# Row-tiled products in two passes: the body's full-height matmuls become pairs of 64-row matmuls on two PSUM banks

## The chip, the cores and the metric

One NeuronCore of one Trainium2 chip. The metric is the time of one execution on the device in microseconds (us). The kernel before takes 799.0 us, the median of three runs (797.24, 799.0 and 799.35).

## The reference

For each of eight batches (3200 tokens, 256 channels, inputs `u`, `v`, `z` in float32):

```
attn = relu(z z^T / S) ** 2            # 3200 x 3200, z has 64 columns
x    = u * (attn @ v)                  # gated attention
wq, wk = x @ w_q, x @ w_k              # 64 columns each
mixed  = (wq wk^T / sqrt(64)) @ x      # = wq @ (wk^T x), a 64 x 256 matrix in the middle
out    = relu(mixed) @ w_out
```

Two shapes of product matter here. The scores `z z^T` and the product with `wk^T x` contract over 64 values, which is half the height of TensorE's array of 128 rows. All others contract over 128 at a time.

## The kernel before

A batch's 25 blocks of 128 tokens are cut into seven groups of output columns: six of 512 tokens and one of 128 (`widths`, `LASTG` is the last). A *score tile* is a block of 128 tokens against one group. Since the scores are symmetric, a tile is made once and its mirror image is got from it by a transposing DMA (`is_turned`, tiles `tt` and `ttl`).

The work runs in **phases**, numbered `k`, in the `while groups` loop (L644 to L767); the order inside a phase is written by hand, and each engine works through its own instructions in that order. One phase does the following.

- **Scores** (`scores`, L212, matmul on L218). Three pairs of score tiles, one after the other at the head of the phase. The two tiles of a pair use the lower and the upper 64 rows of the array (`half = h * dqk`), because `zT` holds `z` twice, once in each half, and they write two PSUM banks of one `sc` tile. In 40 phases a `mix` (L431, also 64 rows) takes the place of one pair.
- **First stage** (`first_stage`, L233): relu and scale from PSUM into a float32 tile `g`. One pair of the phase is done by ScalarE (L237), the others by VectorE (L241).
- **Second stage** (`second_stage`, L247): the squares of the pairs of the phase before, as fp16 tiles `at`, on GpSimd (L256) or ScalarE (L254), then the transposing DMA (L275).
- **Second product** (`second_product`, L287, matmul on L296): blocks of `at`, `tt` or `ttl` as weights and `v` as moving operand, 256 columns a matmul, over all 128 rows. The sums of a group's four 128-token blocks stay in two PSUM banks, `acc0` and `acc1` (pool `pacc`, one buffer each), over the group's one to six phases.
- **An extra**, in about half of the phases: after the first ten matmuls of the second product comes either `keys_and_heads` (L568: `projections` on L344, `heads` on L382, in a few cases `side_mix` or `side_proj`) or `proj` (L472). Each takes a `ps` tile of two banks from a pool of three (`pps`) that the score pairs also use.

When a group closes, the matmuls for `acc0` are put ahead of those for `acc1`, and **the gate** (`gate`, L318, VectorE on L322) multiplies each bank by `u` as soon as that bank is finished. `heads` needs the keys `kx`, which a transposing DMA (`turn_keys`, L364) and a GpSimd copy (`double_keys`, L371) prepare from an earlier extra.

Of the kernel before, what the change touches and what calls it, by code (L numbers as in the profile page):

```python
# [9 lines left out]
FP16 = mybir.dt.float16  # L10
# [6 lines left out]
def kernel(  # L17
# [194 lines left out]
    def scores(p0):  # L212
        pair = tiles[p0 : p0 + 2]
        sc = ps_tile("sc")
        for h, (b, gi, ti) in enumerate(pair):
            gs, gw = starts[gi], widths[gi]
            half = h * dqk
            nc.tensor.matmul(  # L218
                out=sc[:, h, 0:gw],
                lhsT=zT[b][half : half + dqk, ts(ti, P)],  # L220
                rhs=zT[b][half : half + dqk, ds(gs, gw)],
                start=True,
                stop=True,
            )
        return sc
# [7 lines left out]
    def first_stage(p0, sc, on_act):  # L233
        g = pg.tile([P, 2, W], FP32, tag="g", name="g")
        for hs, w in pieces(p0):
            if on_act:
                nc.scalar.activation(  # L237
                    out=g[:, hs, 0:w], in_=sc[:, hs, 0:w], func=RELU, scale=GSCALE
                )
            else:  # L240
                nc.vector.tensor_scalar(  # L241
                    out=g[:, hs, 0:w], in0=sc[:, hs, 0:w], scalar1=0.0,
                    scalar2=GSCALE, op0=AOP.max, op1=AOP.mult,
                )
        return g
# [33 lines left out]
    def weights(b, gi, ti, j):  # L279

        if (b, gi, ti) in made:
            at, at0 = made[b, gi, ti]
            return at[:, ds(at0 + j * P, P)]
        gj = group_of(ti)
        return turned[b, gj, gi][:, j, ti - starts[gj] // P, :]

    def second_product(b, gi, rows_, first, last):  # L287

        nj = widths[gi] // P
        halves = range((nj + 1) // 2)  # L290
        if first:
            for half in halves:
                accs[half] = acc_tile(half, f"acc{half}")

        def one(ti, j):
            nc.tensor.matmul(  # L296
                out=accs[j // 2][:, ds((j % 2) * D, D)],
                lhsT=weights(b, gi, ti, j),
                rhs=vs[b][:, ti, :],
                start=(first and ti == rows_[0] and j % 2 == 0),  # L300
                stop=(last and ti == rows_[-1] and (j % 2 == 1 or j == nj - 1)),
            )

        todo = []
        if last:
            for half in halves:
                for ti in rows_:
                    for j in range(2 * half, min(2 * half + 2, nj)):
                        todo.append(lambda ti=ti, j=j: one(ti, j))
                run = todo.pop()  # L310
                todo.append(lambda run=run, half=half: (run(), gate(b, gi, half)))
        else:
            for ti in rows_:
                for j in range(nj):
                    todo.append(lambda ti=ti, j=j: one(ti, j))
        return todo

    def gate(b, gi, half):  # L318
        if half == 0:
            xs[b, gi] = px.tile([P, 4, D], FP16, tag="x_sb", name="x_sb")  # L320
        n = min(2, widths[gi] // P - 2 * half)
        nc.vector.tensor_mul(  # L322
            out=xs[b, gi][:, 2 * half : 2 * half + n, :].rearrange("p n d -> p (n d)"),
            in0=accs[half][:, 0 : n * D],
            in1=us[b, gi][:, 2 * half : 2 * half + n, :].rearrange("p n d -> p (n d)"),
        )
        if 2 * half + n == widths[gi] // P:
            us.pop((b, gi))
            turn_x(b, gi)
# [10 lines left out]
    def projections(b, gi, w, out, start=True):  # L340

        gw = widths[gi]
        for ac in range(ND):
            nc.tensor.matmul(  # L344
                out=out,
                lhsT=w[:, ac, :, :].rearrange("p t h -> p (t h)"),
                rhs=xTs[b, gi][:, 0 : gw // P, ac, :],
                start=(start and ac == 0),
                stop=(ac == ND - 1),
            )  # L350

# [26 lines left out]
    def heads(b, gis, ps, stop=True):  # L378

        parts = [(gi, n) for gi in gis for n in range(widths[gi] // P)]  # L380
        for gi, n in parts:
            nc.tensor.matmul(  # L382
                out=ps[:, 1, 0:D],
                lhsT=ks[b, gi][:, n, :, :].rearrange("p a h -> p (a h)"),
                rhs=xs[b, gi][:, n, :],
                start=((gi, n) == parts[0]),
                stop=(stop and (gi, n) == parts[-1]),
            )

# [77 lines left out]

    def proj_half(b, gi, banks, half):
        js = range(2 * half, min(2 * half + 2, widths[gi] // P))
        for dc in range(ND):  # L470
            for j in js:
                nc.tensor.matmul(  # L472
                    out=banks[half][:, ds((j % 2) * D, D)],
                    lhsT=rts[b, gi][:, dc, ts(j, P)],
                    rhs=wo[:, dc, :],
                    start=(dc == 0 and j == js[0]),
                    stop=(dc == ND - 1 and j == js[-1]),
                )
# [39 lines left out]
    def side_mix(b, ps):  # L518
        for db in range(ND):
            nc.tensor.matmul(  # L520
                out=ps[:, 1, ds(D + db * P, P)],
                lhsT=hz[b % 2][:, ds(db * P, P)],
                rhs=qks[b, LASTG][:, 0:P],
                start=False,
                stop=(db == ND - 1),
            )

# [8 lines left out]
    def side_proj(b, ps):  # L536
        for dc in range(ND):
            nc.tensor.matmul(
                out=ps[:, 1, D : 2 * D],
                lhsT=rts[b, LASTG][:, dc, :],  # L540
                rhs=wo[:, dc, :],
                start=False,
                stop=(dc == ND - 1),
            )

# [21 lines left out]

    def keys_and_heads(b, gis):  # L568
# [4 lines left out]
        projections(b, gis[0], w, outs[0])  # L573
        aside = None
        if keyed:
            heads(*keyed[0], ps, stop=(len(gis) == 1 and not side))
            if len(gis) > 1:
                projections(b, gis[1], w, outs[1], start=False)
            elif side:
                aside = side.pop(0)  # L580
                aside[0](aside[2], ps)
        for gi, o in zip(gis, outs):
            projections_out(b, gi, o)
            turn_keys(b, gi)
        if keyed:
            hb, hgis = keyed.pop(0)
            heads_out(hb, hgis, ps)
            if hgis[-1] == LASTG:
                mixed_at[0] = max(mixed_at[0], now[0] - 1)
                todo_mix.extend((hb, i, db) for i in range(LASTG // 2) for db in range(ND))  # L590
                side.append((side_mix, side_mix_out, hb))
        if aside:
            aside[1](aside[2], ps)
        keyed.append((b, gis))
        keyed_at[0] = now[0]
# [46 lines left out]
    left, sizes = None, []  # L642
    gate_pending = False
    while groups:  # L644
# [17 lines left out]
        fresh = []  # L662
        for p0 in range(produced, produced + n, 2):
            fresh.append((p0, scores(p0)))
# [12 lines left out]
        for i, (p0, sc) in enumerate(fresh):  # L677
            on_act = i == act_pair and not mixing
            staged.append((p0, first_stage(p0, sc, on_act)))
        if k < 3:  # L680
            turn_first(k + 1)
# [48 lines left out]
        matmuls = second_product(b, gi, rows_, begins, closes)  # L730
        extra = None
        if mixing and todo_proj:
            mb, mg = todo_proj.pop(0)

            def extra():
                proj_out(mb, mg, proj(mb, mg), [(False, nc.sync, widths[mg] // P)])
        elif keying:
            extra = todo_between.pop(0)[1]
        elif len(groups) <= NG and todo_proj and gi < LASTG:
            mb, mg = todo_proj.pop(0)  # L740

            def extra():
                proj_out(mb, mg, proj(mb, mg), [(False, nc.sync, widths[mg] // P)])
        cut = 10 if extra else 0
        if closes and (b, gi) == (last, LASTG):
            assert not extra
            cut = 20

            def extra():
                last_gram(last, LASTG - 1, psg)  # L750

            psg = [acc_tile(1, "xtx")[:, 0:D], ps_tile("xtx")[:, 0, 0:D]]
        for fn in matmuls[:cut]:
            fn()
        if extra:
            extra()
        for x in acts[1:]:
            second_stage(*x)
        for fn in matmuls[cut:]:
            fn()  # L760
        if closes:
            group_done(k, b, gi)
# [15 lines left out]
    def query(gi, o):  # L778
        projections(last, gi, wq2, o)
# [8 lines left out]
    heads(hb, hgis, psh, stop=False)  # L788
# [59 lines left out]
```

## Time and profile before

| | |
|---|---|
| median of the runs | 799.0 us |
| profiled execution, first to last instruction (its span) | 796.6 us |
| matmuls and weight loads on TensorE | 6746 and 6746 |
| TensorE busy | 783.4 us, 98% of the span |
| VectorE, ScalarE, GpSimd busy | 485.5, 462.1, 476.1 us |
| granted TensorE clock | 0.999 |

The profiled execution has one time of its own, the span of its only core; the runs' times lie 0.6 to 2.8 us above it. Engines are PE (TensorE matmul), PEld (its weight load), DVE (VectorE), ACT (ScalarE), POOL (GpSimd) and SP (which issues most DMAs). A matmul's record runs from its start to the modelled arrival of its last column in PSUM, and records of successive matmuls overlap; what one matmul costs the engine is the distance from its start to the next start, not its duration. A group's line gives the count, the busy time, the mean duration in ns, and the idle time before it with what ended it.

### The profile page before, as it was taken

The page shows a single profiled execution, that of the slowest core. Times are in us where ns is not written, and L with a number is a line of the kernel's source. Part 1 is how long each engine was busy: PE and PEld are TensorE (multiplying, and loading weights), DVE is VectorE, ACT ScalarE, POOL GpSimd, SP SyncE. Part 2 cuts the span into 40 slices and gives each one's busy share as a digit, 9 for nine tenths or more (in the row PEclk, how much of TensorE's full clock was granted, in tenths as well). Part 3 has the DMA queues.
Part 4 walks back from the last instruction along what each step waited for, and adds up shares of the span by engine and source line. Part 5 has one row for each costly group of instructions (what it writes and reads, how often), then busy time and mean ns, then how long its engine had stood idle before and what let it go on. Part 6 is the DMA issues. An engine that isn't in the chain of part 4 may idle for free. (4 is left out here: it accounts for less than half of the span.)

```text
span 796.6 us, 16567 instructions
## 1 busy us (share of the span) xinstructions
PE 783.4 (98%) x6746; PEld 584.3 (73%) x6746; DVE 485.5 (61%) x509; ACT 462.1 (58%) x514; POOL 476.1 (60%) x350
## 2 busy tenths in 40 slices
PE   7999999999999999999999999999999999999996
PEld 4777777777777777777777777777777777777784
DVE  5755567646576566655666556775567655675514
ACT  6655556546565557555665556655556655665624
POOL 7967568646664566754667466584566555676420
PEclk9999999999999999999999999999999999999999
DMA  8999899989999989996899978999899995978625
GB/s 170 164 208 191 129 183 161 192 175 173 181 182 202 190 156 174 190 219 146 167 216 165 197 154 182 150 206 222 155 195 177 179 224 117 212 167 192 152 41 221
DMA packets 331116, 141.00 MB, mean 177 GB/s; under 512 B 310560, under 2 KB 313248, under 8 KB 331040
## 3 DMA queue, kind: packets, MB, share of 16 engines
q1 hardware_dynamic: 302768, 123.70, 78.7%
q0 software_dynamic: 28128, 15.98, 18.5%
q8 instruction: 53, 0.87, 0.5%
q10 hardware_dynamic: 144, 0.26, 0.1%
q14 instruction: 23, 0.19, 0.1%
HBM read 59.38 MB, written 26.21 MB: 107 GB/s over the span
## 5 line engine op out<-in xcount | busy, mean ns | idle before, releaser
L256 POOL TENSOR_TENSOR at<-g 128x1024 f16<-128x1024 f32 (+1 forms) x228 | 419.4, 1854 | 223.7 <-DVE g L241 154.2
L241 DVE TENSOR_SCALAR g<-sc 128x1024 f32<-128x1024 f32 (+1 forms) x330 | 376.3, 1183 | 177.2 <-PE sc L218 173.6
L296 PE MATMUL acc<-v_sb,at 128*128 128x256 f16 x3528 | 432.3, 273 | 0.0
L296 PEld LDWEIGHTS <-at 128*128 128x128 f16 x3528 | 332.3, 98 | 104.4 <-issue 60.9
L237 ACT ACTIVATE g<-sc 128x1024 f32<-128x1024 f32 x122 | 125.1, 1025 | 201.7 <-PE sc L218 201.6
L254 ACT ACTIVATE at<-g 128x1024 f16<-128x1024 f32 (+2 forms) x224 | 227.4, 1028 | 0.6 <-DVE g L241 0.6
L296 PE MATMUL acc<-v_sb,tt 128*128 128x256 f16 x1280 | 163.1, 273 | 0.0
L296 PEld LDWEIGHTS <-tt 128*128 128x128 f16 x1280 | 125.2, 98 | 14.5
L218 PE MATMUL sc<-zT 64*128 64x512 f16 x888 | 125.6, 382 | 1.6 <-ACT zT L122 0.9
L322 DVE TENSOR_TENSOR x_sb<-acc,u_sb 128x512 f16<-128x512 f32 (+1 forms) x104 | 69.4, 669 | 76.0 <-PE acc L296 73.3
L452 ACT ACTIVATE rt<-mx 128x1024 f16<-128x1024 f32 x47 | 47.9, 1024 | 65.3 <-PE mx L431 63.5
L218 PEld LDWEIGHTS <-zT 64*128 64x128 f16 x888 | 34.1, 95 | 47.1 <-issue 26.3
L371 POOL COPY kx<-kx 128x256 f16<-128x256 f16 (+1 forms) x54 | 20.1, 378 | 70.3 <-DMA kx<-qk 69.3
L507 ACT ACTIVATE fo<-fo 128x1024 f32<-128x1024 f32 (+2 forms) x44 | 43.8, 1000 | 22.6 <-PE fo L472 22.6
L472 PE MATMUL fo<-wo,rt 128*128 128x256 f16 x384 | 50.0, 273 | 0.1
L472 PEld LDWEIGHTS <-rt 128*128 128x128 f16 x384 | 37.3, 98 | 5.7 <-issue 1.3
L358 ACT CAST qk<-qk 128x512 f16<-128x512 f32 x47 | 27.5, 586 | 21.5 <-PE qk L382 12.6
L395 DVE TENSOR_TENSOR ha<-ha,qk 128x256 f32<-128x256 f32 x31 | 13.1, 421 | 32.0 <-ACT qk L358 25.9
L382 PE MATMUL qk<-x_sb,kx 128*128 128x256 f16 x191 | 28.4, 273 | 0.0
L382 PEld LDWEIGHTS <-kx 128*128 128x128 f16 x195 | 19.1, 98 | 12.0
L296 PE MATMUL acc<-v_sb,ttl 128*128 128x256 f16 x192 | 22.9, 273 | 0.0
L127 POOL DMA_DIRECT2D v_sb<-in_v_dram x35 | 20.8, 596 | 0.0
(61 smaller groups left out, 166.3 us busy)
## 6 DMA issues: line engine op xcount, KB each, us to landing
u_sb<-in_u_dram SPq DMA_DIRECT2D x48, 512.0 KB, 4.7
out_dram<-fo SPq DMA_DIRECT2D x45, 512.0 KB, 3.8
v_sb<-in_v_dram POOLq DMA_DIRECT2D x35, 320.0 KB, 6.2
zd<-in_z_dram POOLq DMA_DIRECT2D x7, 400.0 KB, 9.3
tt<-at SPq DMA_TRANSPOSE x162, 4.4
out_dram<-fo SPq DMA_DIRECT2D x5, 256.0 KB, 2.7
u_sb<-in_u_dram SPq DMA_DIRECT2D x8, 128.0 KB, 3.0
xT_sb<-x_sb SPq DMA_TRANSPOSE x56, 4.1
```

The source lines that it names most:

```text
L218: nc.tensor.matmul(out=sc[:, h, 0:gw], lhsT=zT[b][half : half + dqk, ts(ti, P)], rhs=zT[b][half : half + dqk, ds(gs, gw)], start=True, sto ...
L237: nc.scalar.activation(out=g[:, hs, 0:w], in_=sc[:, hs, 0:w], func=RELU, scale=GSCALE)
L241: nc.vector.tensor_scalar(out=g[:, hs, 0:w], in0=sc[:, hs, 0:w], scalar1=0.0, scalar2=GSCALE, op0=AOP.max, op1=AOP.mult,)
L254: nc.scalar.square(out=out, in_=g[:, hs, 0:w])
L256: nc.gpsimd.tensor_mul(out=out, in0=g[:, hs, 0:w], in1=g[:, hs, 0:w])
L296: nc.tensor.matmul(out=accs[j // 2][:, ds((j % 2) * D, D)], lhsT=weights(b, gi, ti, j), rhs=vs[b][:, ti, :], start=(first and ti == rows_[ ...
L322: nc.vector.tensor_mul(out=xs[b, gi][:, 2 * half : 2 * half + n, :].rearrange("p n d -> p (n d)"), in0=accs[half][:, 0 : n * D], in1=us[b, ...
L358: nc.scalar.copy(out=qks[b, gi][:, 0:gw], in_=out)
L382: nc.tensor.matmul(out=ps[:, 1, 0:D], lhsT=ks[b, gi][:, n, :, :].rearrange("p a h -> p (a h)"), rhs=xs[b, gi][:, n, :], start=((gi, n) == ...
L452: nc.scalar.activation(out=out, in_=ps[:], func=RELU)
L472: nc.tensor.matmul(out=banks[half][:, ds((j % 2) * D, D)], lhsT=rts[b, gi][:, dc, ts(j, P)], rhs=wo[:, dc, :], start=(dc == 0 and j == js[0]),
L507: nc.scalar.mul(out=flat_out[:, sl], in_=part, mul=FINAL_SCALE)
```

## The change

In the phases from the fourth on (`on_lanes`, 159 of 164), every product is made of 64-row matmuls. A product over 128 rows is an `Item` with one PSUM target. `lanes` emits all items of two banks with the lower 64 rows for one bank and the upper 64 rows for the other, interleaved by column position; later the same items are emitted with rows and banks exchanged, so that every bank gets both halves. Between the two passes stands one score pair, which now comes out of the head of the phase (two pairs, or a `mix` and one pair, stay there). `swap_after` makes the first weight load of the second pass wait for the last matmul of each lane of the first pass. From phase to phase the lanes keep their banks (`across`). In the built program this wait stands on a weight load; no instruction is added for it.

The 128-token group needs one PSUM bank only. Except in the last batch it is done in one pass (`is_split`, `both_lanes`): lower rows into `acc0`, upper rows into `acc1`, added up at the gate. An extra goes first in both passes, no longer after ten matmuls of the second product; what reads it follows its second pass. The gate comes after both banks: ScalarE copies `acc1` to SBUF, and VectorE multiplies `acc0` by `u`, then the copy by `u`. Score tiles of the last group are computed at full width (512 columns) and only the last 128 columns are read.

The program has 12268 matmuls in place of 6744 and as many weight loads, 55 more ScalarE copies and 7 more VectorE operations. DMAs are the same in number.

```diff
 def scores(p0):
-            gs, gw = starts[gi], widths[gi]
+            gs = min(starts[gi], S - W)
-                out=sc[:, h, 0:gw],
+                out=sc[:, h, :],
...
+    def lanes(banks, across, second):
+        todo, ends_ = [], {}
+        for lane, rows in enumerate((LOW, HIGH)):
+            at = 0
+            for i in banks[lane ^ across]:
+                todo.append((at, lane, i, rows))
+                at += width(i)
+        for _, lane, i, rows in sorted(todo, key=lambda x: x[:2]):
+            ends_[lane] = i.emit(rows, i.start and not second, i.stop and second)
+        return list(ends_.values())
+
+    def both_lanes(banks):
+        for low, high in zip(*banks):
+            low.emit(LOW, low.start, low.stop)
+            high.emit(HIGH, high.start, high.stop)
+
+    def swap_after(ends_):
+        ins = nc.tensor.nop()
+        for earlier in ends_:
+            tc.add_manual_dep(
+                ins.ins,
+                earlier.ins.name,
+                mybir.DependencyInfo(mybir.DependencyClass.Sync, mybir.DependencyReason.DATA),
+                reason="the lanes change banks",
+            )
+
+    def is_split(b, gi):
+        return gi == LASTG and b + 1 < B
...
+    def gate(b, gi):
...
+        if is_split(b, gi):
+            both = pg.tile([P, W], FP32, tag="g", name="gt")
+            nc.scalar.copy(out=both[:, 0:n], in_=accs[1][:, 0:n])
+            nc.vector.tensor_add(out=both[:, 0:n], in0=accs[0][:, 0:n], in1=both[:, 0:n])
+            nc.vector.tensor_mul(out=x[:, 0:n], in0=both[:, 0:n], in1=ug[:, 0:n])
         else:
+            if nn > 2:
+                upper = pg.tile([P, W], FP32, tag="g", name="gt")
+                nc.scalar.copy(out=upper[:], in_=accs[1][:])
+            nc.vector.tensor_mul(out=x[:, 0:n], in0=accs[0][:, 0:n], in1=ug[:, 0:n])
+            if nn > 2:
+                nc.vector.tensor_mul(out=x[:, n : 2 * n], in0=upper[:], in1=ug[:, n : 2 * n])
+        turn_x(b, gi)
...
-        for p0 in range(produced, produced + n, 2):
-            fresh.append((p0, scores(p0)))
+        pairs = list(range(produced, produced + n, 2))
+        on_lanes = k >= 3 and len(pairs) + bool(mixing) >= 2
+        between_ = [pairs.pop()] if on_lanes else []
+        fresh = [(p0, scores(p0)) for p0 in pairs]
...
+        if on_lanes:
+            split = is_split(b, gi)
+            if extra:
+                ends_ = lanes(extra[0], across, False)
+            if split:
+                both_lanes(banks)
+            else:
+                ends_ = lanes(banks, across, False)
+            for x in acts[1:]:
+                second_stage(*x)
+            for p0 in between_:
+                stage(p0, scores(p0))
+            if extra or not split:
+                swap_after(ends_)
+                across = not across
+            if extra:
+                lanes(extra[0], across, True)
+                extra[1]()
+            if not split:
+                lanes(banks, across, True)
...
         if closes:
+            gate(b, gi)
             group_done(k, b, gi)
```

## The prediction

> **What bounds the kernel now.** I read the page's first part, then who waited for whom, then TensorE's timeline around one score block.
>
> ```profile
> PE 783.4 (98%) x6746; PEld 584.3 (73%) x6746; DVE 485.5 (61%) x509; ACT 462.1 (58%) x514; POOL 476.1 (60%) x350
> ```
>
> TensorE is the bound and no other engine is near. The waits of its matmuls for other engines add up to 7 us. Its weight loads show another idle time, which nobody ends ("issue"):
>
> ```profile
> PEld L296 <- issue: 60.9, 144, 0.4
> PEld L218 <- issue: 26.3, 123, 0.5
> ```
>
> The columns are the total in us, the times and the longest. L296 loads for the second product, L218 for the scores: a gap stands at each change between the two. The timeline of PE shows it from the matmuls' side (start, length, count), then that of PEld at the same place:
>
> ```profile
> 403.11 0.49 PE L296 MATMUL acc<-v_sb,at 128*128 128x256 f16 x3
> 403.54 0.82 PE L218 MATMUL sc<-zT 64*128 64x512 f16 x6
> 404.29 0.39 PE L296 MATMUL acc<-v_sb,at 128*128 128x256 f16 x2
> ```
>
> ```profile
> 403.53 0.12 PEld L218 LDWEIGHTS <-zT 64*128 64x128 f16 x4 [0.21 <-issue]
> ```
>
> Three matmuls of 273 ns in 0.49 us: the pitch is 109 ns, so the third starts at 403.33 and the score would be due at 403.44. It comes at 403.54. The last score pair starts at 403.98, the next pair would be due 216 ns later, and L296 starts at 404.29, another 92 ns late; its second matmul follows after 119 ns, not 109, and the second score pair after 226, not 216. From the last full-height matmul to the second one behind a block of three pairs, the trace has 1078 ns; 109 + 3 x 216 + 109 is 866. A change from 128 rows to 64 and back costs **212 ns**. The waits carry it: the product goes on undisturbed between these changes.
>
> **What the change removes.** 159 phases run on lanes, so 158 round trips go (one is left around the whole stretch). 158 x 0.212 = **-33.5 us**.
>
> **The pitch of a pair on lanes.** A full-height matmul of 256 columns becomes two pairs of 64-row matmuls of which each has half of the work, so 109 ns per pair leaves TensorE's work as it was. No row has a pair of 256 columns. The nearest: two score matmuls start 3 to 4 ns apart and a pair of 512 columns takes 216 ns, as one full-height matmul of 512 does (L344: 216). Four score loads go out within 19 ns (the line of PEld above), so loads of the two halves don't queue for each other. A pair needs four instructions in 109 ns, 27 ns each:
>
> ```profile
> L520 PE MATMUL qk<-ql,hz 128*128 128x128 f16 x14 | 1.9, 219 | 0.0
> ```
>
> These fourteen come in seven couples; 1.9 us by seven is 274 ns, so a couple's second starts 55 ns after the first, load included: the same 27 ns, if only for a few instructions. The bounds are 0 (the score row) and +10 ns a pair (the 119 ns row, where weights could not be loaded ahead). I take **0**, the score row, since it has the same shape of work. There are about 5600 pairs (4883 of the second product, the rest extras), so each ns is 5.6 us: +56 at the upper end.
>
> **The gate.** Now the next group's first matmul needs both accumulator banks, and both are released late:
>
> ```profile
> L322 DVE TENSOR_TENSOR x_sb<-acc,u_sb 128x512 f16<-128x512 f32 x96 | 66.0, 689 | 66.1 <-PE acc L296 63.4 <-DMA ttl<-at 0.7
> ...
> L358 ACT CAST qk<-qk 128x512 f16<-128x512 f32 x47 | 27.5, 586 | 21.5 <-PE qk L382 12.6
> ```
>
> From the start of a group's last matmul: it ends after 273 ns, VectorE starts 37 later, takes 689, and TensorE starts 53 after VectorE's end (all measured): `acc0` is free at 1.05 us. ScalarE's copy of `acc1` (nearest row 586, L358) frees it at 0.95. Before, three score pairs with both switches covered this (first matmul on `acc0` at 0.95 us, on `acc1` at 1.17) and `acc0` was multiplied earlier anyway. Now two pairs stand there, without switches: 109 + 2 x 216 = 541 ns. In the built order,
> - 23 groups begin behind a 512-token group without an extra: 23 x 0.51 = 11.8 us;
> - 24 begin with an extra of at least 1024 columns a lane (436 ns): 24 x 0.07 = 1.7;
> - 7 follow a one-pass (128-token) group. There the score pair of the middle stands behind all matmuls, and VectorE takes its relu (1.22 us, starts at 0.53) before the gate's sum (0.42): `acc0` is free at 2.2 us, and with the output extra in that phase at 2.9. Waits of 1.0 to 1.5 us: 8.3;
> - the last 128-token group, after the lanes: 0.9.
>
> Together **+22.7 us**. VectorE and ScalarE must be idle when a group closes; by the order they are (the middle pair's relu ends about 0.3 us before the gate), and if not, it costs more.
>
> **The swap.** The wait of the second pass stands behind a score pair. Last matmul at 0, score at 109, next due at 325. The last matmul's end is seen at 273 + 40 to 55, so the load comes at 313 to 328 and the matmul 5 ns later; then one pitch is 10 longer, as after a switch. 155 swaps x 14 ns = **+2.2** (0 to 8). Queued behind this load is all of TensorE.
>
> **What becomes late next.** These places had cover before:
> - *Keys.* An extra stands first in its phase instead of after ten matmuls, 1.6 us earlier, and its results leave about 0.5 us later. `heads` needs `kx`:
>
> ```profile
> POOL kx L371 <- DMA kx<-qk: 69.3, 20, 8.1
> ```
>
>   GpSimd waits long for these transposes. In 8 of 54 cases its copy ended less than 2.1 us ahead of the first load; what is missing adds up to 6 us. Bounds 0 and 10, I take **+5**.
> - *PSUM tiles of the extras.* A phase's second score pair takes the tile that the extra of the phase before used. In short phases with two squares on ScalarE (1.05 each, after a 1.02 `mix` output) the extra's output ends at 4.6 us, and the pair is due at 4.4: about 10 places x 0.3 = **+3** (0 to 6).
> - *Unequal lanes.* The extras' two banks differ by 9984 columns in all; at 109 ns per 256 that is 4.3 us if the shorter lane idles in both passes, 0 if the second pass makes up for the first. **+3**, since the swap waits for the longer lane.
> - *Squares.* A pass goes through the blocks twice as fast, so the third pair's `at` is due 1.4 us earlier. First uses had 4.8 us (ScalarE) and 7.1 us (GpSimd) in the median, 2.3 and 3.4 at the lowest twentieth: **+1** (0 to 3).
>
> Free: the wider scores of the last group (8 tiles; the other lane takes 512 columns anyway), 55 ScalarE copies and 7 VectorE operations (58 and 61% busy), 0.7 MB more instructions.
>
> **Sum.** -33.5 + 22.7 + 2.2 + 5 + 3 + 3 + 1 = +3.4. On the profiled span, 796.6 + 3.4 = 800.0; the median of the runs stands 2.4 above that span: **802.4**, say 802. The saving is real, and the gate and the later waits eat it.
>
> **Rivals.**
> 1. *Only the gate and the swap are left over* (faster). The waits put at 5, 3, 3 and 1 share their causes: each stall of TensorE gives ScalarE, GpSimd and the DMAs time, so the next is shorter. -33.5 + 22.7 + 2.2 = -8.6: **790**. For it: the median slacks above. It decides if the four are under 3 us together; with some gates covered too, down to 785.
> 2. *Lanes do not reach 109 ns* (slower). If four instructions per 109 ns, or two loads, cannot be kept up and every pair costs what the first behind a switch does (119), it is 802 + 56 = **858**; from 3 ns a pair on the result is slower by 2% whatever else happens. For it: no row shows this rate for more than a few instructions, and the rate held over long stretches is 54 ns an instruction. Against it: the score pairs and the couples of L520. The Trainium skill, TensorE: Matmul & The Clock Gate, section Back-to-back issue gap, gives about 81 ns for each load and matmul of 128 columns in a sustained stream. By that page a pair would take 162 ns and 5600 pairs some 297 us more, an estimate. The couples' 55 ns disagree with it as far as they go.
> 3. *ScalarE or GpSimd fall behind around the gates* (slower): the copies delay the squares of the same phase, and the next group waits for them too. At 0.25 us for each of 56 groups, +14: **816**. Against it: both have 40% idle time.
> 4. *The switch cost stays*, because a load that waits for the whole array empties it as a switch does: 155 x 0.2 instead of 2.2 is +29: **831**. Against it: the load is due 12 ns after that end anyway.
>
> **How the numbers follow.** Forecast 802: 0.40 (its own range 796 to 810); rival 1, 790: 0.30; rival 2: 0.14; rival 3: 0.11; rival 4: 0.05. A measurement of this kernel tells a difference from none at about 0.3%, 2.4 us. Faster than 796.6: rival 1 and the lower edge of the forecast, 0.33. Within 796.6 to 801.4: the middle of the forecast, 0.20. Slower: 0.47. The range reaches from 786 to 822 and leaves out rivals 2 and 4.
>
> **What would show it.** Right: 109 ns from pair to pair on L291 of the changed kernel, 216 from a score pair to the next product, idle time of about 0.5 us in front of the first matmul of 23 groups, ended by VectorE, about 1 us behind the one-pass groups, and nothing over 20 ns at the swaps. Wrong: a pitch over 110 ns (rival 2), 0.1 to 0.2 us at each swap (rival 4), or no idle time at the gates; then VectorE was done earlier than I worked out, and the time is near 780.

## The result, and the profile after

| | before | after |
|---|---|---|
| median of five runs each | 798.6 us (797.24 to 799.35) | **822.6 us** (821.24 to 831.91) |
| ratio, with its 95% interval | | 1.032 (1.028 to 1.037) |
| span of the profiled execution | 796.6 us | 830.1 us (its own time: 831.9) |
| granted TensorE clock in it | 0.999 | 0.991 |

The kernel is 24 us slower; 802 us was forecast, with a range of 786 to 822. The median before is of five runs; the 799.0 us above was that of the first three. The profiled execution is the slowest of the five, so its sum is made against its own span: 33.5 us more than before. The same kernel profiled once more (`e0_again`) had a span of 825.2 us.

The first line of the page shows what has changed place. TensorE (PE) is no longer busy throughout:

```profile
PE 775.4 (93%) x12270; PEld 625.9 (75%) x12270; DVE 511.8 (62%) x516; ACT 486.5 (59%) x569; POOL 480.6 (58%) x350
```

The waits of PE name who it is idle for (total in us, times, longest):

```profile
PE fo L291 <- ACT rt L512: 15.3, 20, 1.0
PE qk L291 <- POOL kx L429: 9.5, 4, 3.4
PE acc L291 <- DVE x_sb L382: 5.4, 15, 0.4
...
PE qk L291 <- DVE g L241: 2.7, 3, 0.9
PE acc L291 <- ACT gt L381: 2.4, 8, 0.3
PE sc L218 <- DVE g L241: 2.2, 3, 0.7
PE acc L291 <- DVE gt L376: 1.2, 1, 1.2
```

This view counts from the modelled end of the matmul before (273 ns after its start), but the engine could have started the next one after 109 ns, so each wait costs 0.16 us more than it shows: the first row is 15.3 + 20 x 0.16 = 18.5 us. Waits shorter than 0.16 us are not in it at all. So I took the starts of all matmuls, with a pitch of 109 ns for 256 columns and 55 and 216 for 128 and 512, and split the span, without the 7.2 us at its end where TensorE has no more to do, in three:

| us | TensorE idle | one lane of two at work | whole array or both lanes |
|---|---|---|---|
| before | 46.3 | 3.8 | 739.3 |
| after | 71.1 | 20.2 | 731.6 |
| difference | +24.8 | +16.4 | -7.7 |

The three differences add up to the 33.5 us. The idle time by what ended it, in us:

| | before | after | predicted change |
|---|---|---|---|
| switches between 128 and 64 rows, with the long pitch behind them | 32.9 | 0 | -33.5 |
| first matmul of a group, for either bank of the accumulators | 0 | 13.9 (39 waits) | +22.7 |
| score or keys' tile behind a one-pass group, for VectorE's relu | 0 | 6.1 (8 waits) | +3, elsewhere |
| swaps, with the long pitch behind them | 0 | 2.8 | +2.2 |
| **output product, for ScalarE's mix output** | 0 | **18.5** (20 waits) | **not in the sum** |
| keys, for GpSimd's copy | 0 | 10.4 (7 waits) | +5 |
| half clock behind the three longest waits | 0 | about 5 | not in the sum |
| squares | 0 | 1.0 | +1 |
| one lane at work, at half the rate | | +8.2 | +3 |

Two single waits of 1.1 us are not in the table: one for the transposing DMA of `x_sb` in front of the keys' projection (at 47 us), one without a shown releaser (at 162 us). With them the column of after, less the 32.9, is +35.3 us, 1.8 more than the spans differ by: the half clock is an estimate, and the pitches are known to 1 ns.

**The missing row.** One of the twenty waits in PE's timeline (start, length, line, count):

```profile
399.83 0.38 PE L491 MATMUL mx<-qk,hs 64*128 64x512 f16 x2
400.04 0.39 PE L218 MATMUL sc<-zT 64*128 64x512 f16 x2
400.26 0.39 PE L291 MATMUL fo<-wo,rt 64*128 64x256 f16 x4
401.33 0.39 PE L291 MATMUL fo<-wo,rt 64*128 64x256 f16 x4 [0.67 <-ACT rt L512]
401.56 0.38 PE L291 MATMUL acc<-v_sb,at 64*128 64x256 f16 x4
401.77 0.93 PE L291 MATMUL acc<-v_sb,tt 64*128 64x256 f16 x14
```

and ScalarE's at the same place:

```profile
400.25 1.02 ACT L512 ACTIVATE rt<-mx 128x1024 f16<-128x1024 f32 x1 [0.49 <-PE mx L491]
```

The `mix` is the first thing in the phase, and ScalarE takes 1.02 us to turn its sums into `rt`. One score pair stands between the `mix` and the output product that reads `rt`, then four of its matmuls that read the older half of `rt`. The fifth would have been due at 400.26 + 0.22 = 400.48 us; it starts at 401.33, 0.85 us late. In the trace of before, two score pairs and ten matmuls stand between the `mix` and the extra (PE, then ACT):

```profile
407.02 0.39 PE L431 MATMUL mx<-qk,hs 64*128 64x512 f16 x2
407.24 0.59 PE L218 MATMUL sc<-zT 64*128 64x512 f16 x4
407.77 1.26 PE L296 MATMUL acc<-v_sb,at 128*128 128x256 f16 x10
408.87 1.04 PE L472 MATMUL fo<-wo,rt 128*128 128x256 f16 x8
```

```profile
407.45 1.02 ACT L452 ACTIVATE rt<-mx 128x1024 f16<-128x1024 f32 x1 [0.51 <-PE mx L431]
```

In 20 phases the output product reads the `rt` that the `mix` of its own phase completes. There its first load of `rt` follows the end of the mix output by only 0.29 us, and the third, the first that reads the new half, by 0.51 us. The extra moves ahead by ten matmuls (1.09 us) and a score pair (0.22 us), so it was bound to wait 0.8 us in each of these phases. The row was there, and I looked at the keys only.

The last line of PE's timeline also answers for the pitch: 14 matmuls are seven pairs in 0.93 us, and less the last pair's 0.27 that is six pitches of **109 ns**, with 14 loads among them. It holds through the whole body.

**The gate**, as worked out: the group's last pair starts at 405.18 (the end of the line at 403.98 us, less 0.27), the next group's first at 406.26, 1.08 us later where 1.05 was predicted:

```profile
403.98 1.47 PE L291 MATMUL acc<-v_sb,tt 64*128 64x256 f16 x24
405.29 0.60 PE L218 MATMUL sc<-zT 64*128 64x512 f16 x4
406.26 0.28 PE L291 MATMUL acc<-v_sb,at 64*128 64x256 f16 x2 [0.38 <-DVE x_sb L382]
```

**The half clock.** In three stretches the granted clock falls. One of them in windows of the page's kind (window, its length, busy time of PE, PEld, DVE, ACT, POOL with counts, PE clock, DMA share, GB/s), with what GpSimd waited for ahead of it:

```profile
270.00:274.00 4.00, 3.88 (x70) 3.27 (x72) 2.65 (x3) 2.03 (x3) 0.27 (x1) 1.00 1.00 272
274.00:279.00 5.00, 1.59 (x26) 0.98 (x22) 1.22 (x1) 1.97 (x3) 0.92 (x2) 1.00 1.15 170
279.00:283.00 4.00, 4.00 (x43) 2.72 (x40) 0.06 (x1) 0.00 (x0) 3.18 (x2) 0.57 0.95 236
```

```profile
278.08 0.39 POOL L429 COPY kx<-kx 128x256 f16<-128x256 f16 x1 [7.81 <-DMA kx<-qk]
```

TensorE waits 3.6 us for the keys, whose transposing DMA lands late, and right behind it the clock is at half for 3.41 us: 43 matmuls in 4 us where 70 went before. A window of half clock costs 3.41 / 2 = 1.7 us where TensorE works all through it. The other two stand behind waits of 2.1 and 2.9 us; these three waits are the longest of the body. The Trainium skill, TensorE: Matmul & The Clock Gate, section Part 1: The HAM clock gate, says that an idle window of about 3.4 us brings the array to half clock and a busy one back. The length agrees (3.41 us); here 2.1 us of waiting were enough.

**Lanes out of step.** In step, a score pair lasts 0.38 us. Here one score comes 0.11 us behind the other, since its lane was that much behind in the pass before, and the lane ahead has nothing to do until the swap:

```profile
130.93 1.47 PE L291 MATMUL acc<-v_sb,at 64*128 64x256 f16 x23
132.24 0.38 PE L218 MATMUL sc<-zT 64*128 64x512 f16 x1
132.24 0.27 PE L291 MATMUL acc<-v_sb,at 64*128 64x256 f16 x1
132.35 0.38 PE L218 MATMUL sc<-zT 64*128 64x512 f16 x1
```

There are 88 such places with 0.1 us each, half of the one-lane time. Some lanes part in an extra with unequal banks, some behind a gate whose two banks come free 0.09 us apart; they stay apart until the swap.

### The profile page after: what moved, and what is told of

Its sections match the earlier page's. It is cut to its first block, busy times and chain, and to the rows that moved or that the text cites. A ratio compares the mean times of both kernels' runs of the same rounds, so it can differ in the third digit from the quotient of the medians.

```text
span 830.1 us, 27709 instructions
## 1 busy us (share of the span) xinstructions
PE 775.4 (93%) x12270; PEld 625.9 (75%) x12270; DVE 511.8 (62%) x516; ACT 486.5 (59%) x569; POOL 480.6 (58%) x350
## 5 line engine op out<-in xcount | busy, mean ns | idle before, releaser
L291 PE MATMUL acc<-v_sb,at 64*128 64x256 f16 (+1 forms) x6995 | 455.9, 271 | 11.1 <-DVE x_sb L382 5.4
L291 PEld LDWEIGHTS <-at 64*128 64x128 f16 (+1 forms) x6995 | 363.1, 94 | 78.5 <-issue 18.7
L291 PE MATMUL acc<-v_sb,tt 64*128 64x256 f16 (+1 forms) x2528 | 178.9, 270 | 0.0
L218 PE MATMUL sc<-zT 64*128 64x512 f16 x888 | 163.2, 381 | 3.7 <-DVE g L241 2.2
L291 PEld LDWEIGHTS <-tt 64*128 64x128 f16 (+1 forms) x2528 | 134.0, 94 | 13.9
L291 PE MATMUL fo<-wo,rt 64*128 64x256 f16 (+1 forms) x704 | 61.6, 271 | 15.3 <-ACT rt L512 15.3
L291 PE MATMUL qk<-x_sb,kx 64*128 64x256 f16 x378 | 57.5, 273 | 12.2 <-POOL kx L429 9.5
L291 PEld LDWEIGHTS <-rt 64*128 64x128 f16 (+1 forms) x704 | 34.4, 94 | 41.4 <-ACT rt L512 20.8
L382 DVE TENSOR_TENSOR x_sb<-acc,u_sb 128x512 f16<-128x512 f32 (+1 forms) x49 | 33.6, 686 | 39.8 <-PE acc L291 39.0
L384 DVE TENSOR_TENSOR x_sb<-gt,u_sb 128x512 f16<-128x512 f32 x48 | 44.5, 928 | 2.5 <-ACT gt L381 2.1
```

The source lines that it names most:

```text
L218: nc.tensor.matmul(out=sc[:, h, :], lhsT=zT[b][half : half + dqk, ts(ti, P)], rhs=zT[b][half : half + dqk, ds(gs, W)], start=True, stop=True,)
L291: return nc.tensor.matmul(out=self.out, lhsT=self.lhsT(rows), rhs=self.rhs(rows), start=start, stop=stop)
L382: nc.vector.tensor_mul(out=x[:, 0:n], in0=accs[0][:, 0:n], in1=ug[:, 0:n])
L384: nc.vector.tensor_mul(out=x[:, n : 2 * n], in0=upper[:], in1=ug[:, n : 2 * n])
```

## The experiments

Ratios are against the kernel before on the same chip (797.7 to 798.7 us), with 95% intervals. Line numbers in the fences are those of the profile of each kernel.

**e0_again.** The changed kernel once more, as the base of the others.

> The changed kernel once more, for a second profile. Its profiled execution spans 830 us, while four other executions took 821 to 823. Theory (the added time is in TensorE's waits at fixed places): 820 to 824 us, with the same waits of 0.5 us ended by the gate and 0.8 to 1.2 us ended by the mix output in front of the output product, and fewer or shorter waits for the keys' copy on GpSimd than the 10 us of the first profile, since these hang on DMA landings. Rival (twice as many instructions are not kept up with): a pitch of a pair above 109 ns in some stretch.

825.0 us, 1.032 (1.028 to 1.036). The twenty waits of the output product are there again with 18.4 us; those for the keys are 5 with 7.3 us in place of 7 with 10.4. What varies most from execution to execution is the keys.

**e1_out_later.** The output product takes a group whose mix was done in an earlier phase, except in the last batch.

```diff
+        had = len(todo_proj)
         if mixing:
...
-        if mixing and todo_proj:
+        if mixing and (had if len(groups) > NG else todo_proj):
```

> One part undone: the output product of a phase with a mix takes a group whose mix outputs are from an earlier mix, no longer the one whose second half leaves ScalarE in the same phase. Theory: the 20 waits for the mix output (18.5 us in the first profile) go and nothing takes their place: 803 to 806 us. Rival (the stalls are needed by ScalarE and GpSimd, and the next wait grows by what this one loses): above 815 us.

822.3 us, 1.028 (1.023 to 1.033). The waits view of PE:

```profile
PE qk L291 <- POOL kx L429: 13.0, 9, 3.1
...
PE fo L291 <- ACT rt L512: 2.1, 3, 0.7
```

The three waits that are left are those of the last batch. The interval overlaps with that of e0: the medians differ by 3 us only. The profiled execution is the fastest of the four (814.6 us; the others took 821.0 to 825.3). Against the profile of e0, 16 us of waits went, those for the keys rose from 7.3 to 14.4 us from start to start, with 6.8 us at half clock, and the span is 12.4 us shorter. So this edit alone brought 12 us where the keys cost 7 us more, and less in the other executions, of which there is no trace. That each wait had given the DMAs of the keys time is likely, not shown.

**e2_keys_behind.** In phases that begin no group, the keys' extra goes behind the second product in the first pass.

```diff
+            ends_ = []
+            behind = bool(extra) and keying and not begins
-            if extra:
+            if extra and not behind:
                 ends_ = lanes(extra[0], across, False)
...
+            if behind:
+                ends_ = ends_ + lanes(extra[0], across, False)
```

> Another part undone: in phases that do not begin a group, the keys' extra stands behind the second product in the first pass. Theory (the waits for the keys' copy on GpSimd come from its place at the head of the phase): these waits go except in phases that begin a group, minus 5 to 10 us against the changed kernel: 812 to 818 us. Rival (the keys' copy is late for another reason): no change, 822 us, and the same waits at the new place.

818.0 us, 1.025 (1.023 to 1.028): the waits for the keys fell to 4 with 2.8 us, and no half clock is left inside the body. Against e0, with 5 such waits and 7.3 us, the place of the keys' extra is worth 5 us by the ratios and 7 by the medians.

**e3_gate_short.** The gate reads eight columns of each bank.

> The disputed cost taken away: the gate reads only 8 columns of each accumulator bank, and multiplies u by u in place of the rest (that part of the computation is left out), so that the banks are released at once. Theory (the gate is a wait of 0.5 us at 23 places and a little more behind the one-pass groups, 14 us in the first profile): 806 to 810 us. Rival (by the prediction's sum, 22.7 us): 799 to 801 us. If the waits only move on to the PSUM tiles of the extras: above 815 us.

827.2 us, 1.035 (1.032 to 1.037): no gain. The waits for the accumulators fell from 13.9 to 1.6 us, and others took their place:

```profile
PE sc L218 <- DVE g L241: 10.3, 11, 1.8
PE qk L291 <- POOL kx L430: 6.8, 5, 2.6
PE qk L291 <- DVE g L241: 5.6, 7, 0.9
```

The edit has VectorE read both operands of its long multiplications from SBUF, and such a multiplication takes longer while GpSimd computes (last section): the first takes 673 to 676 ns where GpSimd computes nothing, and 1154 ns in the mean. VectorE's queue at the gate then holds up the relu of the next score pair, so this kernel doesn't price the gate; it shows that VectorE has no room there.

**e4_out_and_keys.** e1 and e2 together.

> Both moves of e1_out_later and e2_keys_behind together. Theory (the waits for the mix output and for the keys' copy are separate, and e1_out_later gained little because its keys' waits grew to 14 us and let the clock fall): both go, 18 and 7 us, and the half clock with them: 796 to 802 us. Rival (conserved stalls): 812 us or more, with a new long wait in their place.

814.5 us, 1.020 (1.014 to 1.026), with a spread of 11 us: in the profile, of the slowest execution, waits for the keys are back (5 with 13.7 us, the longest 5.5).

**e5_pair_ahead.** e4, and in one-pass groups the score pair of the middle stands ahead of the group's product.

```diff
-            if split:
-                both_lanes(banks)
-            else:
+            if not split:
                 ends_ = lanes(banks, across, False)
...
-            if not split:
+            if split:
+                both_lanes(banks)
+            else:
                 lanes(banks, across, True)
```

> e4_out_and_keys, and in the one-pass phases the middle score pair stands ahead of the second product, so that VectorE has its relu behind it when the group closes. Theory (behind these phases the gate's sum waits for that relu, and the score pairs and the keys' extra of the next phase wait for VectorE too): the four waits of about 0.4 us ended by L376 or more, and those of 1.0 us in front of the keys, go: 4 to 7 us less than e4_out_and_keys. Rival (these waits are VectorE's total load): no difference.

810.9 us, with eight executions from 801.2 to 814.7; 1.012 (1.008 to 1.016). The interval overlaps with that of e4, so the gain isn't shown. The 6.1 us behind VectorE's relu are gone from their places, and 3.2 us (from start to start) came in their stead:

```profile
PE sc L218 <- ACT rt L512: 2.7, 3, 1.1
```

These are three one-pass phases with a `mix` and an output product. The middle pair is the fourth tile of its phase in a pool of three, and it now comes so early that it waits until ScalarE has read the `mix`. The prediction had seen this place (the relu of the middle pair goes ahead of the gate's sum) but put the wait on the accumulators alone.

**e6_gate_pool.** e5 with the gate's second multiplication on GpSimd (`nc.gpsimd.tensor_mul`).

> e5_pair_ahead with the gate's second multiplication, SBUF by SBUF, on GpSimd in place of VectorE. Theory (VectorE is held 1.6 us at each gate, and the next phase's relu and PSUM tiles wait behind it): 2 to 5 us less than e5_pair_ahead, and nothing at the accumulator waits of 0.5 us, since these end with the first multiplication. Rival (GpSimd delays squares and key copies by what it takes on): 2 to 6 us more.

835.6 us, 1.046 (1.043 to 1.049). The group of the moved operation:

```profile
L384 POOL TENSOR_TENSOR x_sb<-gt,u_sb 128x512 f16<-128x512 f32 x48 | 61.1, 1273 | 241.7 <-ACT gt L381 176.3 <-DVE x_sb L382 59.7 <-issue 5.7
```

It waits for ScalarE's copy with the squares and the key copies queued behind it; TensorE then waits for both:

```profile
PE qk L291 <- POOL kx L429: 16.0, 9, 2.6
...
PE acc L291 <- POOL at L256: 10.6, 12, 3.0
```

GpSimd is 59% busy in e5, and 61 us more on it cost 25 us of time: it is what stands in its queue that counts, not the free share.

**e7_keys_always_behind.** e5 with the keys' extra behind in every phase (`behind = bool(extra) and keying`).

> e5_pair_ahead, with the keys' extra behind the second product of the first pass in phases that begin a group as well. Theory (the long waits that are left, up to 5.5 us, are for key copies that land late): they shrink by the 1.3 to 1.9 us by which the first use moves back, and the half clock behind them goes, while 13 gates lose the cover of the extra (13 x 0.4 = 5 us more): 806 to 812 us, with less spread. Rival (it is only the place in the phase): the waits vanish, 800 to 804 us.

808.2 us, 1.013 (1.011 to 1.016): within the intervals of e5. Fewer waits for the keys (3 with 7.5 us) against more for the accumulators, which the extra had covered.

**e8_keys_turned_first.** e7 with the phase's last square, and so its transposing DMA, behind the extra's outputs.

> e7_keys_always_behind, and in phases with the keys' extra ScalarE's second square, and with it the transposing DMA of its tile, stands behind the extra's outputs again, as in the kernel before. Theory (SyncE issues DMAs in order, and the keys' transpose stands behind that of the squares, 4 to 12 us after the cast that it reads): it is issued earlier, the waits for keys go: 5 to 10 us less than e7_keys_always_behind. Rival (landing time under load decides): no difference, or worse by the squares, which become late.

810.2 us, 1.015 (1.011 to 1.019): no gain. One transpose fewer ahead in SyncE's queue doesn't make the keys come in time.

**e9_before_extras_first.** The kernel before, full height, with the extra first (`cut = 0` in place of 10).

> The kernel before, full height, with nothing but this: the extra stands ahead of all of the second product in its phase, not behind ten matmuls (cut = 0). Theory (the place of the extras costs, not the lanes): the output product's first load, 0.29 us behind the mix output in the kernel before, moves 1.1 us ahead and waits 0.8 us at 20 or more places, and a few key copies are late by about 1 us: 815 to 820 us. Rival (these waits come with the lanes): 798 to 801 us.

869.5 us, 1.090 (1.088 to 1.091). The waits of PE:

```profile
PE qk L344 <- DVE g L241: 29.1, 31, 1.0
PE fo L472 <- ACT rt L452: 26.0, 38, 0.7
PE qk L344 <- ACT g L237: 8.9, 12, 0.8
```

The second row looks like the missing one and is another:

```profile
398.91 1.03 PE L472 MATMUL fo<-wo,rt 128*128 128x256 f16 x8 [0.68 <-ACT rt L452]
```

All 38 output products wait here, 0.85 us each and at their first matmul, also the 18 whose `rt` is of an earlier mix (9 us or more earlier in the trace of before). In the changed kernel 20 wait, at the fifth. By the program, the `mix` and two score pairs hold all three `ps` tiles when the extra asks for one, so the first matmul waits until the same ScalarE operation has read the tile of the `mix`. The first and the third row are the same with three score pairs. So this run shows that an extra at the head costs the full-height kernel 71 us, most of it for a PSUM tile; a wait for `rt` would be hidden under that one, and the run does not show whether it comes without lanes.

**e10_gate_half.** e5 without the gate's second multiplication.

> e5_pair_ahead with the gate's second multiplication left out (the upper half of x is not multiplied by u; ScalarE's copy writes it): VectorE is held 0.7 us at a gate, not 1.6. Theory (the accumulator waits end with the first multiplication, and what VectorE does behind it delays only the next relu): the 14 us of waits for the accumulators stay, 0 to 4 us less than e5_pair_ahead. Rival (VectorE's queue at the gate is what the lanes wait for): 8 us less or more.

805.6 us, 1.010 (1.008 to 1.012): waits for the accumulators of 13.2 us after 13.7. The intervals of e5 and e10 overlap; that half a gate less on VectorE is worth anything isn't shown, and the medians differ by 5 us.

**e11_z_earlier** and **e12_z_earlier_keys_behind.** e5 and e7 with the next batch's `zT` transposed three phases earlier.

```diff
-            due(k + later + 9, lambda: double_z(b + 1))
-            due(k + later + 10, lambda: turn_z(b + 1))
+            due(k + later + 6, lambda: double_z(b + 1))
+            due(k + later + 7, lambda: turn_z(b + 1))
```

> e5_pair_ahead with the next batch's z doubled and turned three phases earlier. In the profiles the long waits for keys (up to 5.5 us, then half clock) come once a batch behind this 4 us transpose on SyncE's queue. Theory (the keys' transposes are late because that queue is full there): the waits over 2 us go, 5 to 12 us less than e5_pair_ahead, 799 to 806 us. Rival (it is the transposes' number, not the place): the waits move to other keys and the time stays at 811.

> e7_keys_always_behind with the same change of z. Theory: 799 to 804 us, a little less than e11_z_earlier only if waits for keys are still left there, a little more if the gates that lose the extra's cover weigh more. Rival: no change from 808.

807.7 us, 1.012 (1.010 to 1.014), and 808.2 us, 1.013 (1.011 to 1.014). In e11 the long waits at the old places are gone, but the keys are waited for 11 times with 13.4 us, elsewhere. This long transpose is not what makes the keys late.

**e13_keys_not_awaited** and **e14_pair_keys_not_awaited.** The changed kernel and e5, where `heads` reads fixed weights in place of `kx`.

```diff
-                lhsT=lambda r, gi=gi, n=n: ks[b, gi][r, n, :, :].rearrange("p a h -> p (a h)"),
+                lhsT=lambda r, n=n: wqk[r, n % 2, :, :].rearrange("p t h -> p (t h)"),
```

> The changed kernel with one thing left out: heads takes fixed weights in place of the keys kx (the keys are still made, transposed and copied, but no matmul reads them, so the result leaves the keys out). It measures all that waiting for keys costs in the changed kernel, half clock included. Theory: 7 to 10 us of waits and 3 to 5 us of half clock go: 808 to 814 us. Rival (what TensorE doesn't wait for here, it waits for behind): 818 us or more.

> The same left out of e5_pair_ahead, where the waits for the mix output are gone already. Theory (gate 14, unequal lanes 8 and small waits are all that is left against 30 us saved at the switches): 796 to 801 us, level with the kernel before. Rival: 805 us or more.

e13: 819.8 us, 1.027 (1.024 to 1.029). With the waits of the output product in place, all waits for the keys are worth 3 to 5 us. e14: 802.8 us, 1.006 (1.003 to 1.008). The three largest rows of PE in e14:

```profile
PE acc L291 <- DVE x_sb L382: 5.2, 14, 1.1
PE acc L291 <- POOL at L256: 3.8, 2, 2.1
PE ztp L118 <- ACT zd L109: 3.4, 1, 3.4
```

From e13 to e14 the output product and the one-pass groups, with the keys' extra at its later place, are worth 17 us together (e13 has 18.4 and 6.1 us of these waits); how much of it is the output product's no run tells apart. From e5 to e14 the keys are worth 5 us by the ratios and 8 by the medians. What is left in e14 is 14.2 us at the gates and 19.1 us with one lane at work. Its span is 800.1 us, where TensorE is idle for 40.5 us: less than before by 5.8, the saving less the gates and other waits.

## Why the prediction was wrong

The direction held the largest chance (0.47 for slower) and the size was wrong: 3.4 us were forecast and 24 came, 0.6 us beyond the range.

- **The step that failed is "What becomes late next".** It followed the extra that moves ahead by its keys and its PSUM tile, not by its third input, the `rt` that the `mix` of the same phase makes. That row is 18.5 us in the profile after, found again in e0 and e13, and gone in e1 but for three waits. In the terms of the sum it is a missing term, not a mis-sized one; in time it and the one-pass groups are worth 17 us together (e13 to e14).
- **Keys, +5 (0 to 10):** 10.4 us of waits and about 5 of half clock in the profile, 7.3 in e0. The price by experiment is 3 to 5 us with the other waits in place (e13) and 5 to 8 without them (e5 to e14). As a term it was nearly right; what it lacked was the clock. One working is off: by the 2.1 us that it gives, what is missing in the eight cases adds up to 8.8 us in the trace of before, not to 6; its upper bound of 10 covers that.
- **Switches, -33.5:** right. 32.9 us of idle time and long pitches are gone.
- **Pitch, 0:** right, 109 ns. Rival 2 (858 us) is false. The Trainium skill, TensorE: Matmul & The Clock Gate, section Back-to-back issue gap, has about 81 ns for each load and matmul of 128 columns, from which 162 ns a pair is an estimate. The trace disagrees for pairs of 64-row matmuls of 256 columns: 109.
- **Gate, +22.7:** the step is right at the 23 ordinary places (11.4 us where 11.8 were predicted; 1.08 us from last to first matmul) and too large in the sum, 13.9 us. Behind the seven one-pass groups the size was nearly right, 7.2 us for 8.3, but in six of them the wait stood on the next relu (6.1 us) and not on the accumulators. Together 20.0.
- **Swap, +2.2:** right, 2.8. Rival 4 (831 us, 0.2 us at each) is false; that the time came near its figure is chance.
- **Unequal lanes, +3:** mis-sized, 8.2. I counted columns of extras, not that a lane once behind stays behind until the swap, after a gate too.
- **PSUM tiles, +3, and squares, +1:** no wait for a `ps` tile at the places that I named (three of the waits behind the one-pass groups are for one); 1.0 us for squares.
- **Rival 1 (790 us)** was wrong in its time. Its mechanism, that each stall makes the next shorter, is borne out in part: in the profile of e1 the keys' waits grew by 7 us when 16 us of others went, and the medians fell by 3 us only.
- **Rival 3 (816 us)**, ScalarE or GpSimd late around the gates, isn't what happened: 1.0 us is ended by a square. e3 and e6 show that VectorE and GpSimd would be late with little more work.

With both unforeseen losses and the waits for the keys out, e14 takes 802.8 us. That is near the forecast, but the terms in it differ (the keys are not in it, the gates are less, the lanes more), so it confirms no sum.

**What stays open.** Why the transposes of the keys land late in some executions and not in others: moving the extra (e2, e7), a square (e8) or the long `zT` transpose (e11) moved the waits and didn't end them all. What the wait for `rt` costs by itself stays open too: 3 us between the medians of e0 and e1, 12 between their profiles, 17 together with the one-pass groups. No kernel tried beats the one before; the best whole one, e11, is 1.2% slower, and e5 and e7 can't be told from it.

## What to carry to other kernels

When a step moves ahead, list every input that it reads, and take for each the distance from its writer's end to this reader in the trace of before: a distance smaller than the move is a wait to come, whoever the writer is. A saving on the bound engine is also time that other engines lose, so price the covers that stood in it; when several late inputs stand in a row, removing one shows the next, and only removing them together shows what they were worth. Read waits on a pipelined engine from start to start, since a view that counts from modelled ends leaves out the pitch that was lost under it.

## What the runs showed of the hardware

- In each of the 17 traces all changes of the granted clock lie on one grid of 3.413 us, and what counts is TensorE's idle time within a step of it (between the modelled end of a matmul and the next start). In the body, all 27 steps at full clock with 1.96 us or more of idle time had a step at half clock behind them, and none with 1.90 us or less. A step at half clock had another one behind it where 0.82 us or more of it was idle (6 cases), and none with 0.77 us or less (27). So the place of a wait on the grid decides: in e1 a wait of 3.0 us was split by it and cost no clock, and in e3 two waits of 1.8 and 0.7 us in one step did.
- VectorE's multiplication of 128x512 float32 takes as long with one operand in PSUM (L382) as with both in SBUF (L384), 692 and 693 ns in the median of the profile after (durations as lowest, median and highest):

```profile
L384 DVE TENSOR_TENSOR x_sb<-gt,u_sb x48: 681/693/2042, 27.9 to 807.5; 128x512 f16<-128x512 f32 x48
L382 DVE TENSOR_TENSOR x_sb<-acc,u_sb x49: 424/692/693, 26.9 to 810.4; 128x512 f16<-128x512 f32 x48, 128x256 f16<-128x256 f32 x1
```

  The highest comes from GpSimd. With both operands in SBUF, the 25 that ran while GpSimd computed nothing took 681 to 693 ns; of the 22 during which it computed for a quarter of the time or more, all but one took 726 to 2042 ns. With one operand in PSUM none took over 693 ns, whatever GpSimd did. One of the slowed ones (DVE, then POOL):

```profile
222.70 1.13 DVE L384 TENSOR_TENSOR x_sb<-gt,u_sb 128x512 f16<-128x512 f32 x1
```

```profile
221.39 1.89 POOL L256 TENSOR_TENSOR at<-g 128x1024 f16<-128x1024 f32 x1 [0.52 <-DVE g L241]
```

  The same operation takes 1273 ns on GpSimd in the mean (e6).
- Two row lanes on two PSUM banks work as two engines: they don't keep step, and in these traces neither waits for the other until an instruction needs both. Not even the program's order holds between them: the two `qk` matmuls below stand ahead of all `acc` ones in the program, and the other lane starts its first `acc` matmul 0.21 us before the second `qk`:

```profile
47.83 0.39 PE L291 MATMUL qk<-xT_sb,wqk 64*128 64x512 f16 x1 [0.98 <-DMA xT_sb<-x_sb]
47.84 0.39 PE L291 MATMUL acc<-v_sb,at 64*128 64x256 f16 x2
48.05 0.38 PE L291 MATMUL qk<-xT_sb,wqk 64*128 64x512 f16 x1
```
